# A fused attention and two-layer feed-forward kernel: another order of the loads and stores on the DMA queue

## The chip, the cores and the metric

The kernel runs on one core of a Trainium2 chip. The metric is the time of one execution on the device, in microseconds (us). Three runs of the kernel before gave 1058.79, 1059.04 and 1060.85 us, a median of 1059.04 us.

## The reference

Block-causal attention over 4 batches, 8 heads, 576 positions and head size 64, followed by two feed-forward layers over the 2304 tokens (4 x 576), model width 512 and hidden width 2048. All arrays are float32.

```python
scores = q @ k.T / 8                       # masked by blocks of 64, then softmax
x = softmax(scores) @ v                    # 2304 tokens x 512
h = x @ w_in;  g = h * clip(h + 3, 0, 6) / 6;      x = g @ w_out   # layer 1
h = x @ w_in2; g = h * tanh(softplus(h));          y = g @ w_out2  # layer 2
```

## The kernel before, in words

**Precision.** The matmuls run in the fast 32-bit format fp32r. So each operand is split into a high part (rounded) and a low part (the rest), and each product is three matmuls: high by high, high by low, low by high (L257 to L259, L755 to L757).

**Tiling.** The tokens are cut into 5 blocks j: four of 512 and one of 256. The hidden width is cut into 16 slices f of 128. A *step* is one pair (block, slice). Layer 1 (m = 0) has steps 0 to 79, layer 2 (m = 1) has steps 80 to 159; step n of layer 1 is block n // 16, slice n % 16. For each step TensorE runs `ff_in` (12 matmuls, h of this slice) and, two steps later, `ff_out` (12 matmuls, which add to the four accumulators y of the block). Between them stand the activation and its split: ACT `a` (L267), DVE `c3` (L313), ACT `gh` (L331), POOL `gl` (L338). At the end of a block `evacuate` copies the four y banks out of PSUM (L779 on DVE, L781 on ACT) and queues their stores to x2d.

**Weights.** They arrive as raw 64-bit floats, 512 KB for half a slice. `fetch` (L145) loads one into a `raw` tile, of which there are two. In blocks 1 and 2 of layer 1 (steps 16 to 47) each step narrows one raw half slice of layer 2's weights to a high and a low part (`narrow2`): ACT L157 and POOL L162 read the raw tile, DVE L165 reads it last and combines, DVE L168 combines again, ACT L804 writes the high part, POOL L807 the low part. Both are stored to DRAM (w2d, stores at L855) and reloaded during block 4 (`reload2`, L815). In block 0 the later slices of layer 1's own weights are narrowed in the same way.

**Tokens.** The attention leaves its output in DRAM, as two parts and a reciprocal of the row sums. For each block j of layer 1 the four 128-row tiles k are loaded by `load_x`: `xr` (L214), `xs` (L215), `xn` (L217, two halves). `xs` and `xn` have one buffer, `xr` has two. Later `add_x` (POOL L227) reads `xs`, `mul_x` (DVE L232) reads `xn`, and `split_x` makes the high part (ACT L239) and the low part (DVE L244). For a block that begins at step n, tile k is loaded in step n + XLOAD[m][k] and added, multiplied and split in step n + XSPLIT[m][k]. This text calls a step with such an add a *split step*.

**Order of work.** The order on each engine is written out by hand. For each step the loop at the end walks through `MOE_PLAN[group]`; the names in it stand for the calls above, with a lag in steps. In blocks 1 to 4 of layer 1 the order is w0 (L157), in, w1 (L162), out, xa (L227), xm (L232), w2 (L165), c3 (L313, of the step before), dma, gh (L331), w3 (L168), gl (L338), xh, xl, whi (L804), evac, wlo (L807), a. Each engine runs its own instructions in this order; semaphores hold an instruction until its operands and its buffer are ready.

**The DMA queue.** Every transfer is issued by SP, at the place `dma` of a step. SP too works in order: an issue that waits for a semaphore holds all issues behind it. `calls(stores, dmas)` issues first the stores that are due in this step, then what is in `dmas`: the raw fetch of the next step's weights (or a reload), and after it the token loads.

Of the kernel before, what the change touches and what calls it, by code (L numbers as in the profile page):

```python
# [96 lines left out]
)  # L97
AHEAD = 6
RELOAD = 4
XLOAD = (-11, -10, -7, -4), (-11, -9, -9, -6)  # L100
XSPLIT = (-10, -6, -4, -2), (-10, -8, -7, -1)
END = 0


# [9 lines left out]
def fused_kernel(ctx: ExitStack, tc: tile.TileContext, qT, kT, vv, w1, w2, outT):  # L114
# [33 lines left out]
    def narrow(raw, name, x=None, tag="val", pool=False):  # L148

        low, high = raw[:, :, 0], raw[:, :, 1]  # L150
        x = x or wst.tile([P, 512], F32, tag="q", name=f"b{name}")


        if pool:
            nc.gpsimd.tensor_scalar(x, high.bitcast(F32), REBASE, 1.0, op0=ALU.mult, op1=ALU.mult)
        else:
            nc.scalar.activation(x, high.bitcast(F32), AF.Copy, scale=REBASE)  # L157
        yield

        val = wst.tile([P, 512], F32, tag=tag, name=f"v{name}")  # L160
        bits = val.bitcast(U32)
        nc.gpsimd.tensor_scalar(val, high.bitcast(F32), 0.0, 1.0, op0=ALU.mult, op1=ALU.mult)  # L162
        yield

        nc.vector.scalar_tensor_tensor(  # L165
            bits, low, 29, bits, op0=ALU.logical_shift_right, op1=ALU.bitwise_or)
        yield
        nc.vector.scalar_tensor_tensor(  # L168
            bits, x.bitcast(U32), 3, bits, op0=ALU.logical_shift_left, op1=ALU.bitwise_or)
        yield val  # L170
# [171 lines left out]
    with ExitStack() as late:  # L342
# [271 lines left out]
        def stage(fn):  # L614
            def run(g):
                if 0 <= g < NG:
                    fn(g // 5, TIME[g % 5])
            return run
# [140 lines left out]
    def spare():  # L759
        return m4.tile([P, 512], F32, tag="o", name=f"m{now[0]}")  # L760
# [4 lines left out]
    def put(d, n, *call):  # L765
        d.setdefault(n, []).append(call)

    def store(n, dst, src):
        put(stores, n, nc.sync.dma_start, dst, src)
# [17 lines left out]

    conv, dmas, stores = {}, {}, {}  # L790
    xs = {}, {}, {}, {}

    def narrow2(n):

        f, c = divmod(n, 2)
        dst = w2d[f, :, :, 512 * c:512 * c + 512]
        if f % 8 == 1 and c == 0:

            x = xr.tile([P, 512], F32, tag="xs", name=f"m{now[0]}", bufs=1)
        else:  # L800
            x = spare()
        for val in narrow(raws.pop((1, n)), f"2_{n}", x, ("q", "val")[n % 2]):
            yield
        nc.scalar.activation(x.bitcast(F32R), val, AF.Copy)  # L804
        store(now[0] + 1, dst[0], x)
        yield
        nc.gpsimd.tensor_sub(val.bitcast(F32R), val, x)  # L807
        store(now[0] + 1, dst[1], val)

    def fetch2(n):  # L810
        raws[1, n] = fetch(w2, *divmod(n, 2))
# [5 lines left out]
    for n, (m, j, f) in enumerate(steps):  # L817
        if m == 0 and j == 0 and f >= WMID:
            for c in range(2):
                put(conv, n - 3, weights1_spare, f, c)  # L820
                put(dmas, max(n - AHEAD, 0), fetch1, f, c, True)
        if m == 0 and 1 <= j <= 2:
            i = (j - 1) * FT + f
            put(dmas, n - 1, fetch2, i)
            put(conv, n, narrow2, i)
        if (m, j) == (0, NJ - 1):
            put(dmas, n + RELOAD, reload2, f)
        if f == 0 and n:
            for k in range(KT):
                put(dmas, n + XLOAD[m][k], load_x, m, j, k)  # L830
                i = n + XSPLIT[m][k]
                put(xs[0], i, add_x, m, j, k)
                put(xs[3], i, mul_x, m, j, k)
                put(xs[1], i, split_x, m, j, k, 0)
                put(xs[2], i, split_x, m, j, k, 1)

    now = [0]
    active = {}

    def group(n):  # L840
        m, j, _ = steps[min(n, len(steps) - 1)]
        return 2 if m else min(j, 1)
# [7 lines left out]
    def calls(*ds):  # L850
        def run_stage(n, m):
            if m == group(n):
                for d in ds:
                    for fn, *args in d.pop(n, ()):
                        fn(*args)  # L855
        return run_stage


    def conv_step(i):
        def run_stage(n, m):  # L860
            if m != group(n):
                return
            if i == 0:
                active[n] = [fn(*args) for fn, *args in conv.pop(n, ())]
            for x in active.get(n - 1 if m == 0 and i >= 2 else n, ()):
                next(x, None)
        return run_stage
# [2 lines left out]
        a=stage(act_a), b1=stage(act_b1), b2=stage(act_b2), ln=stage(act_ln),  # L870
        rexp=stage(act_rexp), mul=stage(act_mul), c1=stage(act_c1), c2=stage(act_c2),
        c3=stage(act_c3), gh=stage(act_gh), gl=stage(act_gl), evac=stage(evacuate),
        out=stage(ff_out), dma=calls(stores, dmas), xa=calls(xs[0]), xh=calls(xs[1]), xl=calls(xs[2]), xm=calls(xs[3]),
        w0=conv_step(0), w1=conv_step(1), w2=conv_step(2), w3=conv_step(3),
        whi=conv_step(4), wlo=conv_step(5),
    )
# [1 line left out]
    for n in range(len(steps) + 6):  # L878
        now[0] = n
        for i, plan in enumerate(MOE_PLAN):  # L880
            for name, lag in plan:
                if (name, n - lag) not in begun:
                    stages[name](n - lag, i)
    assert not (dmas or stores or conv or any(xs))


# [37 lines left out]
```

## Time and profile before

| | |
|---|---|
| median of 3 runs | 1059.04 us |
| profiled execution: its own time | 1061.4 us |
| its span on the page | 1059.3 us |
| TensorE (PE) busy | 1001.9 us, 95% |
| POOL / DVE / ACT busy | 567.1 / 611.4 / 519.7 us |
| mean granted TensorE clock | 0.985 of full speed |
| DMA moved | 128.89 MB |

The span runs from the first to the last instruction of the profiled execution. The attention takes about the first 200 us, layer 1 runs from there to about 660 us (block 0 to about 322 us, blocks 1 and 2 to about 523 us), layer 2 fills the rest. TensorE is busy nearly all of the time; what it lacks lies in the attention's first 20 us, in block 0 (200 to 322 us) and in four places between 376 and 526 us.

### The profile page before, as it was taken

To read this page: it belongs to the slowest core of one execution; us is meant where nothing else is said; L and a number is where in the kernel's file an instruction comes from. 1 tells how busy PE (TensorE), PEld (TensorE's weight loads), DVE (VectorE), ACT (ScalarE), POOL (GpSimd) and SP (SyncE) were. 2 spreads that over 40 slices of the span, in tenths; PEclk is the share of its full clock that TensorE was granted. 3 is DMA by queue.
4 is the path that set the end of the run, shared out by engine and by line. 5 is a ranking of instruction groups with operands and counts; after the bars stand their busy time and mean duration, and the time that the engine had idled before them with its cause. 6 is when DMAs were issued, how large, how long until landed. Compare 5 with 4: busy or idle time off the path is not lost.

```text
span 1059.3 us, 14759 instructions
## 1 busy us (share of the span) xinstructions
PE 1001.9 (95%) x5184; PEld 846.1 (80%) x5184; DVE 611.4 (58%) x1039; ACT 519.7 (49%) x1175; POOL 567.1 (54%) x510
## 2 busy tenths in 40 slices
PE   5999999988879989898999999999999999999998
PEld 4988898866558867686788899788888888888897
DVE  7888878778873334433412221765665656565674
ACT  4788888654434434443422233544444544444454
POOL 6555545566755556565522221565565556555544
PEclk9999999999999999998999999999999999999999
DMA  6677677695115655675320089200100100010010
GB/s 175 173 201 198 170 189 207 184 359 188 50 59 195 223 185 196 223 236 183 117 68 25 1 315 360 80 21 1 59 20 1 60 11 11 1 55 6 1 40 20
DMA packets 95641, 128.89 MB, mean 122 GB/s; under 512 B 42320, under 2 KB 54608, under 8 KB 95568
## 3 DMA queue, kind: packets, MB, share of 16 engines
q1 hardware_dynamic: 95568, 127.96, 38.2%
q8 instruction: 40, 0.66, 0.2%
q14 instruction: 33, 0.27, 0.1%
HBM read 83.36 MB, written 35.73 MB: 112 GB/s over the span
## 4 chain that ended last, share of the span: by engine, by line
PE 46%; issue 3%; POOL 3%; ACT 1%; DVE 0%; POOLq 0%; DVEq 0%
PE y L756 8%; PE y L757 8%; PE y L755 8%; PE h L258 7%; PE h L259 7%; PE h L257 7%; POOL gl L338 1%; POOL hq L325 1%; ACT gh L331 1%; POOL xr L227 0%; POOLq L919 0%; DVE q L283 0%; DVE hq L318 0%; DVE e L300 0%; ACT e L269 0%
## 5 line engine op out<-in xcount | busy, mean ns | idle before, releaser
L756 PE MATMUL y<-gl,wh 128*128 128x512 f32 (+1 forms) x640 | 241.1, 377 | 12.0 <-POOL gl L338 12.0
L755 PE MATMUL y<-gh,wh 128*128 128x512 f32 (+1 forms) x640 | 239.6, 374 | 12.5 <-ACT gh L331 7.9
L257 PE MATMUL h<-xh,wh 128*128 128x512 f32 (+1 forms) x640 | 237.5, 371 | 8.2 <-ACT wh L185 7.0
L259 PE MATMUL h<-xh,wl 128*128 128x512 f32 (+1 forms) x640 | 237.9, 372 | 3.8 <-POOL wl L190 3.2
L757 PE MATMUL y<-gh,wl 128*128 128x512 f32 (+1 forms) x640 | 238.3, 372 | 0.0
L258 PE MATMUL h<-xl,wh 128*128 128x512 f32 (+1 forms) x640 | 236.9, 370 | 0.4 <-DVE xl L244 0.4
L338 POOL TENSOR_TENSOR gl<-e,gh 128x512 fp32r<-128x512 f32 (+1 forms) x80 | 97.8, 1222 | 197.9 <-issue 86.0
L338 POOL TENSOR_TENSOR gl<-hq,gh 128x512 fp32r<-128x512 f32 (+1 forms) x80 | 127.6, 1595 | 89.7 <-ACT gh L331 88.9
L756 PEld LDWEIGHTS y<-gl,wh 128*128 128x128 f32 x640 | 122.3, 191 | 40.3 <-POOL gl L338 20.3
L755 PEld LDWEIGHTS y<-gh,wh 128*128 128x128 f32 x640 | 122.3, 191 | 36.0 <-ACT gh L331 10.5
L257 PEld LDWEIGHTS h<-xh,wh 128*128 128x128 f32 x640 | 121.7, 190 | 30.4 <-ACT wh L185 8.6
L325 POOL TENSOR_TENSOR hq<-hq,e 128x512 f32<-128x512 f32 (+1 forms) x80 | 99.5, 1243 | 83.3 <-DVE e L306 82.7
L259 PEld LDWEIGHTS h<-xh,wl 128*128 128x128 f32 x640 | 121.3, 190 | 27.8 <-POOL wl L190 7.7
L757 PEld LDWEIGHTS y<-gh,wl 128*128 128x128 f32 x640 | 122.5, 191 | 20.1
L258 PEld LDWEIGHTS h<-xl,wh 128*128 128x128 f32 x640 | 121.3, 190 | 20.7 <-DVE xl L244 0.6
L276 DVE TENSOR_SCALAR e<-e 128x512 f32<-128x512 f32 (+1 forms) x80 | 33.2, 415 | 144.6 <-ACT e L269 136.6
L269 ACT ACTIVATE e<-h 128x512 f32<-128x512 f32 (+1 forms) x80 | 44.5, 556 | 144.7 <-PE h L259 144.7
L331 ACT ACTIVATE gh<-e 128x512 fp32r<-128x512 f32 (+1 forms) x80 | 47.2, 591 | 129.3 <-DVE e L313 129.3
L313 DVE SCALAR_TENSOR_TENSOR e<-e,h 128x512 f32<-128x512 f32 (+1 forms) x80 | 50.4, 630 | 81.0 <-ACT e L267 81.0
L165 DVE SCALAR_TENSOR_TENSOR v<-raw,v 128x512 uint32<-128x512 uint32 x64 | 43.9, 701 | 78.5 <-POOL v L162 78.5
L569 DVE TENSOR_TENSOR t<-t,t 128x512 fp32r<-128x512 f32 (+2 forms) x144 | 69.9, 522 | 27.2 <-ACT t L564 27.1
L518 ACT ACTIVATE p<-s,nm 128x64 f32<-128x64 f32 (+2 forms) x144 | 75.2, 531 | 14.4 <-DVE nm L507 14.4
(63 smaller groups left out, 1605.4 us busy)
## 6 DMA issues: line engine op xcount, KB each, us to landing
raw<-w SPq DMA_DIRECT2D x64, 512.0 KB
x1d<-x SPq DMA_DIRECT2D x64, 144.0 KB
qb<-qs SPq DMA_DIRECT2D x30, 288.0 KB
w2d<-m SPq DMA_DIRECT2D x32, 256.0 KB
w2d<-v SPq DMA_DIRECT2D x32, 256.0 KB
wh<-w2d SPq DMA_DIRECT2D x16, 512.0 KB
wl<-w2d SPq DMA_DIRECT2D x16, 512.0 KB
q<-qT SPq DMA_DIRECT2D x16, 288.0 KB
```

The lines of the kernel that those rows point to most:

```text
L257: nc.tensor.matmul(h[:, :n], hi[:, ws], xh, start=(k == 0), stop=False)
L258: nc.tensor.matmul(h[:, :n], hi[:, ws], xl, start=False, stop=False)
L259: nc.tensor.matmul(h[:, :n], lo[:, ws], xh, start=False, stop=(k == KT - 1))
L313: nc.vector.scalar_tensor_tensor(g, g, 6.0, h, op0=ALU.min, op1=ALU.mult)
L325: nc.gpsimd.tensor_mul(g, g, et.pop((m, j, f)))
L331: nc.scalar.activation(gh, g, AF.Copy)
L338: nc.gpsimd.tensor_sub(gl, g, f32(gh))
L518: nc.scalar.activation(t, sc, AF.Exp, bias=nm[:, c:c + 1], accum_out=su[:, i:i + 1])
L569: nc.vector.tensor_sub(z[:, 1, loc, :], tp, f32(z[:, 0, loc, :]))
L755: nc.tensor.matmul(y, hi[:, ws], gh, start=first, stop=False)
L756: nc.tensor.matmul(y, hi[:, ws], gl, start=False, stop=False)
L757: nc.tensor.matmul(y, lo[:, ws], gh, start=False, stop=last)
```

## The change

The queue's order in a step becomes `dmas` (raw fetches and reloads), then `stores`, then the token loads, which get a list of their own. The store of the low part of a narrowed weight is issued two steps after its conversion instead of one. Of layer 1's token tiles, k = 1 is loaded 9 steps ahead of its block instead of 10, k = 2 is loaded 6 instead of 7 ahead, and k = 3 is loaded 3 instead of 4 ahead; k = 1 is added and split 7 steps ahead instead of 6. Layer 2's tables are as before.

```diff
-XLOAD = (-11, -10, -7, -4), (-11, -9, -9, -6)
-XSPLIT = (-10, -6, -4, -2), (-10, -8, -7, -1)
+XLOAD = (-11, -9, -6, -3), (-11, -9, -9, -6)
+XSPLIT = (-10, -7, -4, -2), (-10, -8, -7, -1)
...
-    conv, dmas, stores = {}, {}, {}
+    conv, dmas, stores, loads = {}, {}, {}, {}
...
         nc.gpsimd.tensor_sub(val.bitcast(F32R), val, x)
-        store(now[0] + 1, dst[1], val)
+        store(now[0] + 2, dst[1], val)
...
-                put(dmas, n + XLOAD[m][k], load_x, m, j, k)
+                put(loads, n + XLOAD[m][k], load_x, m, j, k)
...
-        out=stage(ff_out), dma=calls(stores, dmas), xa=calls(xs[0]), xh=calls(xs[1]), xl=calls(xs[2]), xm=calls(xs[3]),
+        out=stage(ff_out), dma=calls(dmas, stores, loads), xa=calls(xs[0]), xh=calls(xs[1]), xl=calls(xs[2]), xm=calls(xs[3]),
...
-    assert not (dmas or stores or conv or any(xs))
+    assert not (dmas or loads or stores or conv or any(xs))
```

## Rows read from the trace of the kernel before

**Rows 1.** Windows: span, busy us (instructions) by engine, TensorE clock, DMA share, GB/s.

```profile
260.00:280.00 20.00, 18.01 (x74) 13.21 (x72) 17.90 (x19) 10.47 (x18) 14.33 (x12) 0.99 0.31 116
...
440.00:490.00 50.00, 50.00 (x221) 41.08 (x219) 17.29 (x25) 18.18 (x31) 26.09 (x24) 1.00 0.68 217
```

**Rows 2.** Waits of PE, 322 to 526 us: total us, times, longest us.

```profile
PE y L755 <- ACT gh L331: 5.7, 3, 3.1
PE y L755 <- ACT o L781: 4.5, 1, 4.5
PE y L756 <- POOL gl L338: 4.2, 5, 0.9
```

**Rows 3.** Timeline of POOL, a regular step: start us, duration us, operation [idle before].

```profile
422.16 1.29 POOL L338 TENSOR_TENSOR gl<-e,gh 128x512 fp32r<-128x512 f32 x1 [2.13 <-issue]
...
424.68 0.64 POOL L162 TENSOR_SCALAR v<-raw 128x512 f32<-128x512 f32 x1
427.44 1.29 POOL L338 TENSOR_TENSOR gl<-e,gh 128x512 fp32r<-128x512 f32 x1 [2.13 <-issue]
```

**Rows 4.** Timeline of POOL, steps around splits in block 1.

```profile
398.32 1.29 POOL L338 TENSOR_TENSOR gl<-e,gh 128x512 fp32r<-128x512 f32 x1 [2.73 <-issue]
...
404.04 1.30 POOL L338 TENSOR_TENSOR gl<-e,gh 128x512 fp32r<-128x512 f32 x1 [2.13 <-issue]
...
411.18 1.27 POOL L338 TENSOR_TENSOR gl<-e,gh 128x512 fp32r<-128x512 f32 x1 [2.72 <-issue]
```

**Rows 5.** Timeline of POOL, where it stood idle ahead of L162 or L227.

```profile
341.32 0.65 POOL L162 TENSOR_SCALAR v<-raw 128x512 f32<-128x512 f32 x1 [0.42 <-DMA raw<-w]
...
349.40 1.29 POOL L338 TENSOR_TENSOR gl<-e,gh 128x512 fp32r<-128x512 f32 x1 [2.13 <-issue]
...
354.41 1.29 POOL L227 TENSOR_TENSOR xr<-xr,xs 128x512 f32<-128x512 f32 x1 [1.85 <-DMA xs<-x1d]
...
388.44 0.64 POOL L162 TENSOR_SCALAR v<-raw 128x512 f32<-128x512 f32 x1 [3.60 <-DMA raw<-w]
...
442.24 0.65 POOL L162 TENSOR_SCALAR v<-raw 128x512 f32<-128x512 f32 x1 [1.74 <-ACT e L267]
445.02 1.29 POOL L338 TENSOR_TENSOR gl<-e,gh 128x512 fp32r<-128x512 f32 x1 [2.13 <-issue]
...
454.87 1.29 POOL L227 TENSOR_TENSOR xr<-xr,xs 128x512 f32<-128x512 f32 x1 [1.40 <-DMA xs<-x1d]
...
490.41 0.65 POOL L162 TENSOR_SCALAR v<-raw 128x512 f32<-128x512 f32 x1 [5.09 <-PE h L259]
```

**Rows 6.** Timeline of SP's queue: start us, issue us, transfer.

```profile
348.03 0.42 SPq L215 DMA_DIRECT2D xs<-x1d  x1
...
379.18 0.32 SPq L215 DMA_DIRECT2D xs<-x1d  x1
...
382.14 0.51 SPq L145 DMA_DIRECT2D raw<-w  x1
...
430.43 0.37 SPq L145 DMA_DIRECT2D raw<-w  x1
```

**Rows 7.** Timeline of ACT at the end of block 1.

```profile
431.93 0.63 ACT L331 ACTIVATE gh<-e 128x512 fp32r<-128x512 f32 x1 [2.26 <-DVE e L313]
...
433.07 1.07 ACT L781 ACTIVATE o<-y 128x512 f32<-128x512 f32 x2
```

**Rows 8.** Timeline of PE, single matmuls of steps 20, 32, 35, 40 and 48.

```profile
354.75 0.39 PE L756 MATMUL y<-gl,wh 128*128 128x512 f32 x1
...
433.70 0.50 PE L755 MATMUL y<-gh,wh 128*128 128x512 f32 x1 [4.53 <-ACT o L781]
...
451.99 0.39 PE L756 MATMUL y<-gl,wh 128*128 128x512 f32 x1
...
478.96 0.39 PE L755 MATMUL y<-gh,wh 128*128 128x512 f32 x1
...
531.03 0.39 PE L755 MATMUL y<-gh,wh 128*128 128x512 f32 x1
```

## The prediction, made before the changed kernel had run

> **What bounds the kernel now.** I read the page's slices first: TensorE is busy 95% of the span, so a gain can only come from its stalls. The change touches nothing ahead of layer 1's block 0, so I looked at the waits of PE from step 16 on (322 us). There is little: it stood 14.4 us, for `gh`, for `gl`, and once 4.5 us for an accumulator that ACT had not yet copied out [rows 2]. Each of these is late work of the elementwise engines, so the next view is the timeline of POOL, the busiest of them there.
>
> It shows a closed chain. `gl` of a step is followed on POOL by `wlo` (L807) and by `w1` (L162) of the next step; on DVE w2 (L165) waits for that `w1`, `c3` stands behind w2, `gh` needs `c3`, and the next `gl` needs `gh`. So each `gl` depends on the one before through the weights' conversion. From `gl` to `gl` a regular step takes 427.44 - 422.16 = 5.28 us [rows 3]. TensorE's own step is 24 matmuls; 221 matmuls in 50.00 us [rows 1] make 0.226 us each and 5.43 us a step. A regular step thus lets the chain gain 0.15 us. A split step puts `add_x` between `w1` and w2: 411.18 - 404.04 = 7.14 us, 1.71 us more than TensorE's step; the step behind it takes 404.04 - 398.32 = 5.72 us, 0.29 us more [rows 4].
>
> What else the chain loses shows as idle time of POOL ahead of L162 or L227. There are six such places in steps 16 to 47: 0.42, 1.85 and 3.60 us in block 1, and 1.74, 1.40 and 5.09 us in block 2 [rows 5]. The rows name a raw tile or `xs` in four of them. In the other two an ACT and a PE instruction are named, but L162 needs neither result; the raw tile of that step lands just before, so I count them as raw waits too. Block 1 loses 5.87 us, block 2 loses 8.23 us.
>
> SP's queue says why. The issue of `xs` at 379.18 [rows 6] was held until the add of tile k = 1, since `xs` has one buffer and k = 2 was loaded a step before that add. The raw fetch behind it went out at 382.14, and its tile brought the 3.60 us. The 5.09 us in block 2 is the same place one block later. In regular steps too the fetch stands behind the store of the low part, hence behind L807: at 430.43 [rows 6], though the last reader of its buffer (L165 of the step before) was done before the `gl` at 427.44 [rows 3]. That is 3 us or more lost in each step.
>
> **The change part by part.** *Fetch first.* The fetch now waits only for L165 of the step before, and goes out at least 3 us earlier (above). All four raw waits go: 0.42 + 3.60 + 1.74 + 5.09 = 10.85 us off the chain. Nothing is added; the fetch moves past the two stores of its step and, in one step a block, past four x2d stores. These still go out in the step after `evacuate`; they are read at least 50 steps later.
>
> *k = 1 and k = 2 at other steps.* Now each load comes one step or more after the add and multiply of the tile before, so SP isn't held by it. The number of split steps stays four a block. k = 1 is split a step earlier: same instructions, same chain, cost nil. In block 0 the same move shifts one split from step 10 to step 9 where DVE is busy 17.90 of 20 us [rows 1], so one step gets longer and the next shorter; I take nil, with 1.5 us either way for where it falls.
>
> *Low part a step later.* It takes the wait for L807 off SP. The value's buffer is held one step longer. Four buffers (two tags of two) alternate, so it is next written three regular steps (15.8 us) after its L807; the store now goes out about 5.3 us after that, so some 10 us are left for the landing. Cost nil; without that cover each excess us would stop L162 by as much, in every step.
>
> *Token loads last.* They now stand behind the fetch and two stores of their step. But they needn't wait for L807 either, only for the high store (ACT, before L807): about 2.6 us earlier than today (L807 1.3, and the issues of low store and fetch). Today `xs` of k = 0 is issued at 348.03 and its add begins at 354.41, 6.4 us later [rows 5, 6]. Without waits that add could begin 1.85 us sooner, at 352.6; issued at about 345.4 the tile has 7.2 us. So I take the 1.85 and 1.40 us as gone; from nothing of it to all is the bound. k = 3, now loaded one step ahead of its add, has the same 7.2 us.
>
> A rule of the Trainium skill speaks against this part: DMA: Bandwidth & Descriptors, "Queues, rings and completion order", says that each DMA engine takes a ring's descriptors in order. By it, a tile behind 1 MB of fetch and stores lands after them. The 6.4 us above, measured behind a fetch, doesn't contradict it. That outcome is rival 1.
>
> *The reload order.* In layer 1's last block reloads now precede stores of the same step; only step 83 has both. Nil: x2d is not read soon.
>
> **What becomes of the 14.10 us.** Not all of it reaches the end; TensorE also waits for the chain itself. Follow how far `gl` runs ahead of its matmul. At step 20 `gl` starts at 349.40 and its L756 at 354.75 [rows 5, 8]; `gl` takes 1.3 us, so 4.05 us are in hand, after the change 4.05 + 0.42 = 4.47. Block 1's splits then cost, up to the fourth, 4 x 1.71 + 3 x 0.29 - 2 x 0.15 = 7.41, and 0.29 behind it: 7.70 us. So TensorE still loses about 7.70 - 4.47 = 3.2 us there, in small pieces. At the block's end it still stops for the accumulators: ACT copies after `gh` of the chain, and TensorE resumes 433.70 - 431.93 = 1.77 us after that `gh` [rows 7, 8]. Both before and after, that moment is set by the chain. So the whole 5.87 us of block 1 arrives there: the matmul at 433.70 starts at 427.83.
>
> In block 2 TensorE has the reserve that this stop gives. At step 35: 451.99 - 445.02 - 1.3 = 5.67 us [rows 5, 8], and 5.67 + 1.74 = 7.41 after the change. The splits again cost 7.70, less 0.15 for the regular step in between: 7.55. So 0.1 to 0.3 us of stall are left where today steps 40 to 48 take 531.03 - 478.96 = 52.07 us against 8 x 5.43 = 43.44 [rows 8]: 8.6 us of stalls and half-clock matmuls. Gain 8.4 us.
>
> The stop at the block's end is followed by a stretch at half clock, in steps 32 to 40: (478.96 - 433.70) - 43.44 = 1.8 us [rows 8]. I leave it as it is.
>
> Sum: 5.87 + 8.4 = 14.3 us. The profiled execution's 1061.4 us (span 1059.3) become 1047.1; it lay 2.4 us above the median, so the median goes from 1059.04 to **1044.8 us**.
>
> **The rivals.**
> 1. *Tokens late.* Behind fetch and stores the k = 0 and k = 3 tiles land as late as k = 0 does now, in both blocks. For: the two waits for `xs` [rows 5]. Against: the earlier issue. Price 2 x (1.85 + 1.40) = 6.5 us: 1051.3.
> 2. *The stalls go altogether.* If the chain isn't as rigid as I read it, the small stalls (3.2), the stop for the accumulators (4.5), its half clock (1.8) and 0.2 go as well: 1035.1. For: the instructions involved are short. Against: in regular steps the period repeats at 5.28 us, and ACT's place behind `gh` isn't changed.
> 3. *It doesn't do what it says.* The raws are late because the DMA engines are full, not because of the issue. Then only the two long holds shrink, say half of 3.60 + 5.09: about 1055. Against: the DMA share is 0.68 in a long stretch of such steps [rows 1].
> 4. *Slower.* The same queue as in rival 1, but the four one-step tiles (k = 0 and k = 3 of two blocks) land so late that POOL waits more than 14.3 / 4 = 3.6 us for each: landing over 7.2 + 3.6 = 10.8 us after issue, against at most 6.4 today. At 4.5 us each: 1044.8 + 18 = 1062.8.
>
> **How the numbers follow.** Forecast (1042 to 1048) 0.72, tokens late 0.11, stalls gone in whole or part (below 1042) 0.10, little effect 0.04, slower 0.03. The range is 1040 to 1052: it takes in the forecast, block 0's 1.5 us, late tokens, and the better part of rival 2's small pieces. Less than 0.2% (2.1 us) can't be told from no change. Faster by more than that: 0.95; within it 0.02; slower 0.03.
>
> **What would show it.** Right: no idle POOL ahead of L162 in steps 16 to 47; SP never held at an `xs` of layer 1's blocks 2 and 3; `gl` to `gl` at 5.3, 7.1 and 5.7 us only; a stop of some 4.5 us left at the end of block 1, and none over 0.5 us in block 2. Wrong: a wait for `xs` or `xn` ahead of L227 or L232 (rival 1), no stop at the block's end (rival 2), raw tiles still awaited (rival 3).

## The result, and the profile after

The changed kernel takes 1049.88 us (median of 5 runs, 1046.73 to 1052.01) against 1059.04 us before; the ratio is 0.9914, 95% interval 0.989 to 0.9937. Timed again beside other kernels it gave 1049.04 us and a ratio of 0.9905 (0.9889 to 0.992). So it is faster by 9.2 us in the first and 10.5 us in the second timing (from 1059.49 us), where 14.3 us were forecast: inside the range of 1040 to 1052 us, but above the forecast's own 1042 to 1048 us. The profiled execution took 1052.01 us, the longest of its five runs.

The page of the changed kernel: span, busy time by engine, granted clock in 40 slices.

```profile
span 1049.6 us, 14743 instructions
...
PE 1001.7 (95%) x5184; PEld 848.0 (81%) x5184; DVE 610.8 (58%) x1039; ACT 517.6 (49%) x1175; POOL 566.7 (54%) x510
...
PEclk9999999989998999899999999999999999999999
```

The waits of POOL from 322 to 526 us in the changed kernel (total us, times, longest us; `issue` stands where the profile shows nothing that the engine waited for):

```profile
POOL gl L338 <- issue: 76.4, 31, 4.5
POOL gl L338 <- ACT gh L331: 7.5, 2, 4.1
POOL v L807 <- ACT m L804: 2.3, 1, 2.3
POOL gl L338 <- PE y L756: 0.6, 1, 0.6
```

No line names L162 or L227 any more: the six waits of [rows 5], 14.10 us in all, are gone, raw tiles and tokens alike. What POOL still waits for stands ahead of `gl` and L807, in its own chain. The timeline of POOL shows that chain unchanged:

```profile
347.11 1.30 POOL L338 TENSOR_TENSOR gl<-e,gh 128x512 fp32r<-128x512 f32 x1 [2.13 <-issue]
...
352.39 1.31 POOL L338 TENSOR_TENSOR gl<-e,gh 128x512 fp32r<-128x512 f32 x1 [2.13 <-issue]
...
355.51 1.31 POOL L227 TENSOR_TENSOR xr<-xr,xs 128x512 f32<-128x512 f32 x1
359.54 1.29 POOL L338 TENSOR_TENSOR gl<-e,gh 128x512 fp32r<-128x512 f32 x1 [2.72 <-issue]
...
365.27 1.29 POOL L338 TENSOR_TENSOR gl<-e,gh 128x512 fp32r<-128x512 f32 x1 [2.13 <-issue]
```

From `gl` to `gl` it takes 5.28, 7.15 and 5.73 us, as in [rows 3, 4]. Two steps stray from these three values: 7.69 us at the end of block 0, taken up below, and 6.27 us at the end of block 1, where ACT's L157 waits 3.0 us. Block 2's reserve covers the second: TensorE has no wait there. The add at 355.51 (k = 0 of block 2) follows L162 at once, where it stood 1.85 us before; its `xs` was issued at 348.49, 7.0 us ahead.

TensorE's waits in the same stretch, and its matmuls that answer to [rows 8] (the first of step 16, one each of the `ff_out` of steps 20, 32 and 40, the first of step 48, the first of its `ff_out`):

```profile
PE y L755 <- ACT o L781: 4.5, 1, 4.5
PE y L756 <- POOL gl L338: 2.7, 3, 0.9
PE y L755 <- ACT gh L331: 0.2, 1, 0.2
```

```profile
322.82 0.63 PE L257 MATMUL h<-xh,wh 128*128 128x512 f32 x1
...
356.22 0.39 PE L756 MATMUL y<-gl,wh 128*128 128x512 f32 x1
...
431.15 0.80 PE L755 MATMUL y<-gh,wh 128*128 128x512 f32 x1 [4.51 <-ACT o L781]
...
477.32 0.39 PE L755 MATMUL y<-gh,wh 128*128 128x512 f32 x1
...
507.37 0.39 PE L257 MATMUL h<-xh,wh 128*128 128x512 f32 x1
...
521.25 0.39 PE L755 MATMUL y<-gh,wh 128*128 128x512 f32 x1
```

The stop at the end of block 1 stands (4.51 us, before 4.53), and from step 40 to 48 it is 521.25 - 477.32 = 43.93 us, where full speed is 43.44: block 2's stalls are gone. The measure used below is the distance from the first matmul of step 16 to the first of step 48. It holds all that the change can reach and leaves block 0 and layer 2 out. Here it is 507.37 - 322.82 = 184.55 us. In the kernel before:

```profile
321.86 0.39 PE L257 MATMUL h<-xh,wh 128*128 128x512 f32 x1
...
517.10 0.39 PE L257 MATMUL h<-xh,wh 128*128 128x512 f32 x1
```

195.24 us, so 10.7 us were gained, not 14.3. The span shrank by 9.7 us, since block 0 and the attention took 1.0 us more in this execution (in a second profile of the changed kernel 0.7 us less).

**Where the rest went.** The reserve of `gl` at step 20 was to be 4.47 us; it is 356.22 - 352.39 - 1.3 = 2.5 us. It was lost at the end of block 0. There DVE copies two of the four accumulators (L779) into tiles shared with the weights' high parts. In the changed kernel:

```profile
328.17 0.68 DVE L779 TENSOR_SCALAR o<-y 128x512 f32<-128x512 f32 x1
333.46 0.69 DVE L779 TENSOR_SCALAR o<-y 128x512 f32<-128x512 f32 x1 [4.60 <-DMA w2d<-m]
```

The second copy waits until the store of an earlier high part (`w2d<-m`) has left its tile. SP's queue just before:

```profile
327.51 0.33 SPq L145 DMA_DIRECT2D raw<-w  x1
327.88 0.43 SPq L855 DMA_DIRECT2D w2d<-v  x1
328.95 0.33 SPq L855 DMA_DIRECT2D w2d<-m  x1
```

The store stands behind a fetch (512 KB) and a low store (256 KB) that went out 1.1 to 1.4 us ahead of it, and frees its tile 333.46 - 328.95 = 4.5 us after its issue. In the kernel before, the same copy and the same store, with the fetch 3.3 us ahead:

```profile
329.74 0.69 DVE L779 TENSOR_SCALAR o<-y 128x512 f32<-128x512 f32 x1 [2.35 <-DMA w2d<-m]
```

```profile
324.17 0.37 SPq L145 DMA_DIRECT2D raw<-w  x1
327.48 0.32 SPq L855 DMA_DIRECT2D w2d<-m  x1
```

329.74 - 327.48 = 2.3 us. DVE stands still in the chain (w2 and `c3` are behind the copy). Two steps later ACT's L157 waits 3.41 us for an x2d store behind the next fetch:

```profile
340.51 0.66 ACT L157 ACTIVATE m<-raw 128x512 f32<-128x512 f32 x1 [3.41 <-DMA x2d<-o]
```

That was 0.39 us before. The second part of the shortfall is TensorE's clock: after the stop at 431 us it ran for 5.4 us at a granted clock of 0.50 (1.2 GHz), before for 3.4 us; steps 32 to 40 took 477.32 - 431.15 = 46.17 us against 45.26.

### The profile page after: what moved, and what is told of

Read it like the earlier page. It is cut to its first block, busy times and chain, and to the rows that moved or that the text cites. A ratio compares the mean times of both kernels' runs of the same rounds, so it can differ in the third digit from the quotient of the medians.

```text
span 1049.6 us, 14743 instructions
## 1 busy us (share of the span) xinstructions
PE 1001.7 (95%) x5184; PEld 848.0 (81%) x5184; DVE 610.8 (58%) x1039; ACT 517.6 (49%) x1175; POOL 566.7 (54%) x510
## 4 chain that ended last, share of the span: by engine, by line
PE 53%; POOL 2%; issue 2%; ACT 1%; DVE 0%; POOLq 0%; DVEq 0%
PE y L756 9%; PE y L757 9%; PE y L755 9%; PE h L258 9%; PE h L259 9%; PE h L257 9%; POOL gl L338 1%; POOL hq L325 1%; ACT gh L331 1%; POOLq L919 0%; DVE q L283 0%; DVE hq L318 0%; ACT e L269 0%; DVE e L300 0%; DVE e L276 0%
## 5 line engine op out<-in xcount | busy, mean ns | idle before, releaser
L269 ACT ACTIVATE e<-h 128x512 f32<-128x512 f32 (+1 forms) x80 | 44.4, 555 | 145.0 <-PE h L259 145.0
L267 ACT ACTIVATE e<-h 128x512 f32<-128x512 f32 (+1 forms) x80 | 43.7, 547 | 84.0 <-PE h L259 80.4
```

Source lines behind the costliest of these rows:

```text
L269: nc.scalar.activation(e, h, AF.Exp)
```

## The experiments

All are timed against the kernel before, on the same chip as it; its median there was 1059.5 to 1060.4 us. "Step 16 to 48" is the measure above, from each kernel's own profile.

**1. The queue order without the token tables.**

```diff
-XLOAD = (-11, -9, -6, -3), (-11, -9, -9, -6)
-XSPLIT = (-10, -7, -4, -2), (-10, -8, -7, -1)
+XLOAD = (-11, -10, -7, -4), (-11, -9, -9, -6)
+XSPLIT = (-10, -6, -4, -2), (-10, -8, -7, -1)
```

> The changed kernel with the token tables of before; the queue order (fetch, stores, tokens) and the late low store stay. Theory A: the raw waits come from the fetch's place in the queue, so this alone gives nearly all of the gain: in steps 16 to 47 POOL's waits ahead of L162 fall from 10.9 us to under 3 us (the two held xs issues remain, but the fetch of that step is already out); time 1050 to 1053 us. Rival B: the long waits (3.60 and 5.09 us) belong to the token tables, so they stay as they are here, and the time is near 1056 us.

Measured: 1053.39 us, ratio 0.9931 (0.9918 to 0.9945); step 16 to 48 in 187.9 us. The only idle POOL ahead of L162 in its timeline:

```profile
387.18 0.66 POOL L162 TENSOR_SCALAR v<-raw 128x512 f32<-128x512 f32 x1 [1.41 <-PE y L756]
...
483.88 0.65 POOL L162 TENSOR_SCALAR v<-raw 128x512 f32<-128x512 f32 x1 [2.12 <-DMA w2d<-m]
```

These are the places of the 3.60 and 5.09 us. SP is still held at `xs`, for 8.3 us at the longest, but the fetch of that step is out already. Theory A holds in kind, a little short: 3.5 us of waits are left where under 3 were expected, and the time lies 0.4 us beyond its range.

**2. The token tables without the queue order.** The kernel before, with the two new tables.

> The kernel before with the new token tables alone; order of the queue and low store as before. Theory A: the two held xs issues go and with them 3.60 and 5.09 us of waits, but fetch and tokens stay behind the low store, so the waits of 0.42, 1.85, 1.74 and 1.40 us stay and k = 3, now loaded one step ahead of its add, adds waits for xs of 1.4 to 1.9 us in each block: about 1053 to 1055 us. Rival B (the tables are the whole gain): about 1050 us and no new wait for xs.

Measured: 1057.9 us, ratio 0.9982 (0.9969 to 0.9994); step 16 to 48 in 193.4 us. That is less gain than either theory said. The long raw waits went, though shorter ones ahead of L162 still make 4.6 us, and POOL now waits in all four one-step token loads:

```profile
POOL xr L227 <- DMA xs<-x1d: 6.1, 4, 2.0
```

So the tables pay little without the order (1.8 us of the stretch, against 187.9 - 184.55 = 3.4 us with it): behind the low store and the fetch, k = 3 comes too late for its new step.

**3. The late low store alone.**

```diff
-        store(now[0] + 1, dst[1], val)
+        store(now[0] + 2, dst[1], val)
```

> The kernel before with the low store a step later, alone. Theory A: SP isn't held for POOL's low part, so the fetch leaves 2 us sooner and tokens too: the waits of 0.42, 1.85, 1.74 and 1.40 us mostly go, while the held xs issues and their 3.60 and 5.09 us stay; 1055 to 1057 us. Rival G: the fetch has to be first for any of it, since the low store still stands ahead of it: no change, 1059 us.

Measured: 1055.32 us, ratio 0.9962 (0.9948 to 0.9975); step 16 to 48 in 190.7 us, 4.6 us less than before. The short waits are gone, the two long ones stay, in POOL's timeline:

```profile
387.52 0.65 POOL L162 TENSOR_SCALAR v<-raw 128x512 f32<-128x512 f32 x1 [5.08 <-DMA raw<-w]
...
485.75 0.65 POOL L162 TENSOR_SCALAR v<-raw 128x512 f32<-128x512 f32 x1 [4.35 <-issue]
```

Theory A as expected. Taking the wait for POOL's low part off SP gives some two fifths of the gain by itself.

**4. High stores ahead of the fetch in every step.** The low store stays behind the fetch.

```diff
-        store(now[0] + 2, dst[1], val)
+        put(lows, now[0] + 2, nc.sync.dma_start, dst[1], val)
...
-        out=stage(ff_out), dma=calls(dmas, stores, loads), ...
+        out=stage(ff_out), dma=calls(stores, dmas, lows, loads), ...
```

> The changed kernel with the stores of high parts and of x2d ahead of the fetch; order: high and x2d stores, fetch, low stores, tokens. Theory A: some 2 us of the missing gain went at the end of block 0, where the copy of the last accumulator on DVE waited 4.60 us (2.35 before) for a buffer held by a high store that now lands behind a fetch and a low store, and L157 waited 3.41 us for an x2d store behind the same. Here these waits are back at 2.4 and 0.4 us, gl of step 19 comes 2 us sooner, block 1 ends 2 us sooner, and the time is about 1048 us. No raw wait comes back, since the fetch has over 7 us to spare. Rival C: the missing gain is half-clock stretches alone, which fall as they fall: the DVE wait may shrink, but the time stays within 1 us of 1049.9.

Measured: 1048.96 us, ratio 0.9902 (0.9886 to 0.9919). Run again beside the changed kernel itself:

> The changed kernel once more, beside the next one on the same chip. Theory A and rival C alike: a median of 1048 to 1051 us; runs differ by up to 5 us, and the run with the higher mean clock is the shorter one.

> The kernel of the third experiment once more, beside the changed kernel on the same chip. Theory A: the two waits at the end of block 0 are short again in the trace and the median is 1 to 3 us under that of the changed kernel. Rival C: the waits are short, but the medians lie within 1 us of each other.

Measured: the changed kernel 1049.04 us, this one 1050.27 us (0.9913, 0.9895 to 0.9931). The waits at the end of block 0 are short in its traces, as theory A said, but the time is not: it lies 1.2 us above the changed kernel's, nearer to rival C (within 1 us) than to theory A (1 to 3 us below). POOL shows why it isn't a clean test: fetch and tokens leave later in their step, and POOL's waits from 322 to 526 us have lines again that the changed kernel lacks. Those of the second run:

```profile
POOL xr L227 <- DMA xs<-x1d: 1.6, 3, 0.6
...
POOL v L162 <- DMA raw<-w: 0.3, 1, 0.3
```

In the first run it is 2.8 us for `xs`, and 0.4 us for a raw tile, which the expectation had ruled out. There the end of block 1 comes 0.8 us sooner than in the changed kernel, but steps 40 to 48 take 45.42 us instead of 43.93: the gain is given back further down the same queue.

**5. Stores first in steps 18 and 19 alone.** This takes the two waits away and leaves the queue as it is in the steps with tokens.

```diff
-                for d in ds:
+                order = (stores, dmas, loads) if len(ds) == 3 and n in (18, 19) else ds
+                for d in order:
```

> The changed kernel, with the stores ahead of the fetch in steps 18 and 19 alone, where block 0's accumulators are copied out; all other steps keep fetch, stores, tokens. Theory A: DVE's wait of 4.6 us for the buffer of the last copy falls to some 2.3 us and L157's wait for the x2d store from 3.4 to under 1 us; the reserve of gl at step 19 (2.3 us in the changed kernel) rises to about 4.3 us, no wait for tokens appears (unlike with high stores first everywhere), and from the first matmul of step 16 to that of step 48 it takes about 182.2 us instead of 183.9 to 184.6; median 1047 to 1048.5 us. Rival C: the waits shrink, but the stretch from step 16 to 48 stays above 183.5 us, since the stall at block 1's end or half-clock stretches take it back.

Measured: 1047.54 us, ratio 0.9879 (0.9864 to 0.9894). DVE's second copy, `gl` of step 20, and TensorE's matmuls (the first of step 16, of the `ff_out` of steps 20 and 32, the first of step 48):

```profile
328.74 0.69 DVE L779 TENSOR_SCALAR o<-y 128x512 f32<-128x512 f32 x1 [2.37 <-DMA w2d<-m]
```

```profile
347.24 1.30 POOL L338 TENSOR_TENSOR gl<-e,gh 128x512 fp32r<-128x512 f32 x1 [2.13 <-issue]
```

```profile
319.78 0.39 PE L257 MATMUL h<-xh,wh 128*128 128x512 f32 x1
...
352.65 0.39 PE L756 MATMUL y<-gl,wh 128*128 128x512 f32 x1
...
425.98 0.80 PE L755 MATMUL y<-gh,wh 128*128 128x512 f32 x1 [4.49 <-ACT o L781]
...
502.41 0.39 PE L257 MATMUL h<-xh,wh 128*128 128x512 f32 x1
```

The first matmuls of steps 16 and 48 in the second profile of the changed kernel:

```profile
321.17 0.40 PE L257 MATMUL h<-xh,wh 128*128 128x512 f32 x1
...
505.04 0.39 PE L257 MATMUL h<-xh,wh 128*128 128x512 f32 x1
```

From step 16 to 48 it takes 182.63 us, against 184.55 in the changed kernel and 183.87 in its second profile. The reserve of `gl` at step 20 is 352.65 - 347.24 - 1.3 = 4.1 us, where the changed kernel had 2.5. The end of block 1 comes 425.98 - 319.78 = 106.20 us after the start of step 16, in the kernel before 433.70 - 321.86 = 111.84: 5.64 us sooner, of the 5.87 forecast. POOL has no wait for tokens here. Theory A holds: the two waits cost 1.2 to 1.9 us of this stretch. The medians alone would hardly show it, since the interval touches that of the changed kernel's second timing (0.9894 and 0.9889).

**6. The low part on DVE.** The changed kernel, with the subtraction of L807 moved off POOL.

```diff
-        nc.gpsimd.tensor_sub(val.bitcast(F32R), val, x)
+        nc.vector.tensor_sub(val.bitcast(F32R), val, x)
```

> The changed kernel with the low part of layer 2's weights subtracted on DVE instead of POOL (L807's place). Theory A: POOL's chain gl, wlo, w1, w2, c3, gh sets the pace of block 1 in the changed kernel too; without wlo a regular step is some 1.25 us shorter (about 4.0 us), so TensorE sets the pace: the small stalls of block 1 (5.9 us) go, the stop at its end (4.7 us) shrinks under 2 us, and the time falls by 7 to 12 us to 1038 to 1043 us. Rival D: another chain, through DVE or ACT, takes over at about the same length (DVE now waits in order for ACT's high part), or the accumulator's stop is as long as before: at most 3 us gained.

Measured: 1036.4 us, ratio 0.9779 (0.9764 to 0.9794), with experiment 8 the fastest. POOL's timeline:

```profile
357.35 1.29 POOL L338 TENSOR_TENSOR gl<-e,gh 128x512 fp32r<-128x512 f32 x1 [2.75 <-DMA raw<-w]
...
362.25 1.30 POOL L338 TENSOR_TENSOR gl<-e,gh 128x512 fp32r<-128x512 f32 x1 [2.55 <-issue]
363.50 1.11 POOL L162 TENSOR_SCALAR v<-raw 128x512 f32<-128x512 f32 x1
366.73 1.30 POOL L338 TENSOR_TENSOR gl<-e,gh 128x512 fp32r<-128x512 f32 x1 [2.12 <-DMA w2d<-m]
...
373.06 1.30 POOL L338 TENSOR_TENSOR gl<-e,gh 128x512 fp32r<-128x512 f32 x1 [2.72 <-issue]
```

A regular step takes 4.48 us, a split step 6.33, the one behind it 4.90: the reserve now grows faster than the splits use it up. TensorE's groups of matmuls from 322 to 526 us (busy us, mean ns, idle before) show no idle time:

```profile
L257 PE MATMUL h<-xh,wh 128*128 128x512 f32 x152 | 59.4, 391 | 0.0
...
L755 PE MATMUL y<-gh,wh 128*128 128x512 f32 x147 | 57.3, 390 | 0.1
```

Step 16 to 48 takes 172.1 us, 12.5 us less than in the changed kernel. So the chain on POOL was indeed what held TensorE in the changed kernel, small stalls and stop at the block's end alike.

**7. The same on the kernel before**, with its old queue and tables.

> The kernel before, its queue order and its token tables, with the low part of layer 2's weights subtracted on DVE. Theory A: with the short chain TensorE has 2 to 7 us in hand, which take up most of the raw and token waits, so the queue is worth little here: 1036 to 1041 us. Rival F: the waits behind the queue reach TensorE whatever the chain's length, and the queue change keeps its worth: about 1046 us.

Measured: 1049.06 us, ratio 0.9896 (0.9877 to 0.9914); step 16 to 48 in 181.7 us. Here theory A was wrong and rival F nearer, though the time lies 3 us above its 1046: the reserve doesn't swallow the waits. POOL still stands where the fetch was held:

```profile
384.10 0.64 POOL L162 TENSOR_SCALAR v<-raw 128x512 f32<-128x512 f32 x1 [5.17 <-PE y L756]
```

With the short chain the queue change is worth 1049.06 - 1036.4 = 12.7 us by the medians and 181.7 - 172.1 = 9.6 us of the stretch, about as much as with the long one (9.2 to 10.5 and 10.7). A shorter chain reaches each raw tile sooner, and the old queue then makes it wait more often: this wait included, 15 waits ahead of L162 make 26.7 us, against 4 of 10.85 us before.

**8. Both: low part on DVE, and stores first in steps 18 and 19.**

> The kernel of the fourth experiment (low part on DVE) with the stores first in steps 18 and 19. Theory A: there TensorE doesn't wait in blocks 1 and 2 at all, so the shorter waits only add to a reserve that is never used up: 1036.4 us, within 1.5 us. Rival H: some of the time from step 16 to 48 (172.1 us there) still hangs on the end of block 0: 2 us less.

Measured: 1036.75 us, ratio 0.9776 (0.9759 to 0.9794); step 16 to 48 in 171.8 us. As theory A said, nothing is left to gain there.

## Why the prediction was right, and where it was too high

- *What bounds the kernel: right.* The closed chain through POOL, with 5.28, 7.14 and 5.72 us, was there after the change to 0.01 us, and experiment 6 shows that it held TensorE.
- *Fetch first: right.* All four raw waits went. Experiments 1 and 3 divide the credit: the late low store removes the short ones, the fetch's place most of the long ones, the tables the last 1.41 and 2.12 us.
- *Token loads last: right.* No wait for `xs` or `xn` was left; rival 1 didn't come about. In another place a transfer did come late behind others: a high store behind a fetch and a low store freed its tile after 4.5 us instead of 2.3. That agrees with the rule of the Trainium skill that I set against this part (DMA: Bandwidth & Descriptors, "Queues, rings and completion order"), by which each DMA engine takes a ring's descriptors in order.
- *The step that failed* is in "Fetch first": "Nothing is added; the fetch moves past the two stores of its step". I asked who reads the stored data next, and not who needs the buffer back. At the end of block 0 the accumulators' copies need it at once. That cost the reserve 2 us, and through the chain the end of block 1: it came 3.5 us sooner (4.0 in the second profile), not 5.87. With the stores first in steps 18 and 19 (experiment 5) it comes 5.64 us sooner, and step 16 to 48 gains 12.6 us of the 14.3. Of the 3.6 us that are missing from this stretch in the changed kernel, these are 2.4; the half clock is 0.9, block 2 is 0.3.
- *Block 2: right* (8.4 us forecast as the gain from step 40 to 48; 52.07 - 43.93 = 8.1 measured).
- *The range: in part luck.* The median lies nearer to rival 1's 1051.3 us than to 1044.8, though no token was late. The range reached up to 1052 for late tokens and for block 0, and so took in a cost that the prediction had put at nothing.
- *"I leave it as it is"*, of the half clock behind the stop: wrong by 0.9 us in the profile above. The half clock also goes with the spread of the runs: the changed kernel's longest, 1052.01 us, has a mean granted clock of 0.984, its shortest, 1046.73 us, of 0.992. The changed kernel and experiment 5 have the same code up to step 17, and the kernel before differs from them there only in block 0's token steps; yet they part in the window from 318 to 326 us (columns as in [rows 1]). The kernel before, the changed kernel and experiment 5:

```profile
318.00:326.00 8.00, 8.00 (x30) 6.41 (x29) 2.58 (x4) 2.44 (x5) 3.79 (x4) 0.79 0.28 91
```

```profile
318.00:326.00 8.00, 8.00 (x23) 6.43 (x24) 2.08 (x3) 1.62 (x3) 3.78 (x4) 0.63 0.28 100
```

```profile
318.00:326.00 8.00, 8.00 (x37) 6.63 (x36) 3.51 (x6) 2.76 (x6) 3.60 (x5) 1.00 0.37 133
```

30, 23 and 37 matmuls in the same 8 us, by granted clocks of 0.79, 0.63 and 1.00. Block 0 took 119.9, 120.6 and 118.4 us in these three. So up to 2 us of a single comparison of whole executions can be where the clock fell, not the kernel. What sets where it falls stays open.

## What to carry to other kernels

When a transfer is moved ahead in a queue, list for every transfer that it passes both who needs its data and who waits for its buffer; the second list is the one that bites, and it bites where buffers are shared, as between a block's end and a running stream. Before valuing removed waits, find the chain that repeats every step, and follow the reserve of the bounding engine step by step: it told which waits reach the end, and pointed at the cheaper cure (one instruction moved to an engine that is less busy there: DVE 17.29 us of 50, POOL 26.09 [rows 1]). And reserve doesn't make a queue's order irrelevant: the faster the chain, the sooner it asks.

## What the runs showed of the hardware

- A 256 KB store from SBUF freed its buffer 2.3 us after issue with 3.3 us of distance to the fetch ahead of it, and 4.5 us after issue with a fetch and a low store 1.1 to 1.4 us ahead.
- POOL's L162 takes 0.64 to 0.65 us in the changed kernel, but 1.08 to 1.11 us in experiment 6, where DVE's subtraction overlaps it in the profile; L807 on POOL took 1.29 us in regular steps and 1.74 us in split steps, beside DVE's split of the tokens (L244). L244 itself took 1.42 us beside POOL's `gl`, where DVE's L232, alone, took 0.69 us. I had put the shorter chain at 4.0 us; these 0.45 us are most of the difference to 4.48. That the two engines hinder each other is an inference; it wasn't tried by itself.
